# Seven products for q and k in two more pairs of tiles, and what moves between VectorE, ScalarE and Pool with it

## The chip, the cores and the metric

The kernel runs on one core of one Trainium2 chip. The core has TensorE (matrix products, called PE in the profile; its weight loads PEld), VectorE (DVE), ScalarE (ACT), GpSimd (POOL) and SyncE (SP), which here only issues DMAs. Each engine works through its own list of instructions in order, and semaphores make it wait for the others. The metric is the time of one execution in microseconds, as the median of several runs. All times below are microseconds unless marked ns.

## The reference

A layer normalisation, a local attention and a two-layer network on the same normalised input, joined by a gate. Cut to what is computed:

```
xn  = layernorm(x)                                  # x: 2048 x 512
q, k, v = xn @ wqkv                                 # 32 heads of 16
logits[s, w] = q[s] . k[s - 2 w] / 4                # 8 keys, every second position, masked before 0
o   = softmax(logits) over w, times v[s - 2 w]
s   = o @ wo
h   = relu(xn @ w1 + b1) ** 2                       # 1792 wide
g   = silu(h @ w2 + b2)
out = x + s * g
```

b2 is drawn 3.8 times larger than the other biases. All inputs and outputs are float32.

## The kernel before, in words

*Precision.* Every operand of a large product is split in a high part, rounded to the product's format by a ScalarE copy, and a low part, the difference, which VectorE or Pool subtracts. A product of two split operands takes three passes (line 34): high x high, high x low, low x high.

*First stage.* The 2048 rows are 16 tiles of 128. Lines 787 to 793 run over pairs of tiles, (0, 1) ahead of the loop, then a = 2, 4, ... 14, and make q, k and v of both tiles. `pair` (line 730) does it straight: six results of 12 products each, 72 in all. `pair_of_seven` (line 744) makes q and k of the two tiles with seven products of half size (six matrix instructions each, a scheme after Strassen), from four sums of input quarters (`copy_quarter`, `sums`, `high_sums`, `low_sums`, lines 489 to 520) and four sums of weights (the buffers T1 to T4), and then joins the products by two ScalarE copies, five VectorE additions and two Pool additions into the staging tiles `stg`; v stays straight. That is 7 x 6 + 24 = 66. `SEVEN` (line 40) says for which pairs. What is to be done beside pair a for later pairs (transposes of the next tiles, their split, the statistics of tiles further on) is listed by step in `plan` (lines 685 to 718). q, k, v go to DRAM and are loaded again in attention's layout; so do the split inputs (`sx`, `xU`) for later chunks.

*Second stage.* Four chunks c of 512 rows (line 870 on). For each of 14 blocks f of the hidden layer, `up(c, f)` (line 575) makes 12 products into `ph`, ScalarE writes the Relu, the square rounded (`h`, high) and the square in full; in chunk 0 the full square stays in PSUM and VectorE subtracts (`lowh`, line 595), in later chunks it goes to the tile `hf`, of which there is one buffer, and Pool subtracts. Two blocks later `down` (line 802) makes 12 products into the four accumulators `pb`. Between them stand the attention's output products `pw` (`out_product`). When a chunk ends, `gate` (line 847) adds b2 to each `pb` and takes the Silu; `finish` (line 858) multiplies by `pw`, adds x and stores. The order of TensorE at such a boundary is: the last `pb` products, `up` 0 and 1 of the next chunk, one `pw`, `up` 2, and then `pb` with h 0, whose third product is the first that reads a low part.

*Weights of the network.* `next_w` (line 388) prepares one block of w1 and w2: two ScalarE copies, two Pool subtractions, and the load of the raw block two further on. `ahead` (line 720) says at which steps of the first stage blocks are prepared; the rest follow one per step of chunk 0. Blocks that are named in `HOME` (line 38) take a buffer that the first stage used for its weights (Q0 to V1, T1 to T4), and so must wait for that buffer's last use.

*The order on VectorE.* The attention (a generator, line 238) fills what the other work leaves of VectorE: eight units of 256 rows, per unit four times a product of k and q and a reduction, a softmax, and four times a product with v and a reduction. `pump` (line 365) emits its instructions as long as the planner's VectorE clock, which adds a price per instruction (line 61), is not past the TensorE clock plus a margin. `not_before` sets the VectorE clock forward where an instruction depends on TensorE. The engines keep the order of emission, ScalarE's and Pool's too; loads by `dma` alone are placed by the framework. In the softmax's second half (`soft_b`, line 287) VectorE makes the sums and reciprocals and Pool scales `L`.

Of the kernel before, what the change touches and what calls it, by code (L numbers as in the profile page):

```python
# [8 lines left out]
F32 = mybir.dt.float32  # L9
FR = mybir.dt.float32r  # L10
AF = mybir.ActivationFunctionType
# [3 lines left out]
P = 128  # L15
# [10 lines left out]
NCH = S // C  # L26
TPC = C // P
# [7 lines left out]


Q0, Q1, K0, K1, V0, V1, T1, T2, T3, T4 = range(10)
HOME = {0: 10, 1: T1, 2: T2, 3: T3, 4: T4, 5: Q0, 6: Q1, 7: K0, 8: K1, 9: V0, 10: V1}

SEVEN = range(4, 12, 2)  # L40

WARM = 18
WARM2 = 3
# [2 lines left out]

STATS = 6

MATMUL, TRANSPOSE, DVE_FIXED, SLACK, LATE, ROOM0, ROOM = 227, 150, 170, 500, 3000, 500, 3500

BEHIND, FREE, LAND, LOAD = 5000, 2000, 4500, 10500

# [2 lines left out]
def body(ctx: ExitStack, tc: tile.TileContext, x, wqkv, wo, w1, b1, w2, b2, out):  # L55
# [3 lines left out]
    clock = {"PE": 0.0, "V": 0.0}  # L59

    def price(engine, name, a, k):
        if engine == "PE":
            return MATMUL if name == "matmul" else TRANSPOSE
        ap = k["in_"] if name == "tensor_reduce" else k.get("out", a[0] if a else None)
        n = 1
        for d in ap.shape[1:]:
            n *= d
        if name == "reciprocal":
            n *= 8
        return n / 0.96 + DVE_FIXED  # L70

    class Ordered:

# [14 lines left out]
    PE, V, A, G = Ordered(nc.tensor, "PE"), Ordered(nc.vector, "V"), Ordered(nc.scalar), Ordered(nc.gpsimd)  # L88

    def not_before(t):  # L90
        clock["V"] = max(clock["V"], t)
# [3 lines left out]
    def queue(out, in_):  # L95

        tc.keep_in_program_order(dma(out, in_))
# [7 lines left out]
    hpool = ctx.enter_context(tc.tile_pool(name="ph", bufs=1))  # L105
# [5 lines left out]
    def psH(name):  # L111
        return psum.tile([P, 512], F32, name=name, tag="h", bufs=2)

    def psT(name):
        return psum.tile([P, 512], F32, name=name, tag="tp", bufs=2)
# [33 lines left out]
    def buffer(name, i):  # L149
        return wts.tile([P, 2, 2, 512], FR, name=name, tag=f"b{i}")  # L150
# [237 lines left out]
    def next_w():  # L388

        f = len(w12)  # L390
        if f < NF:
            w12[f] = buffer(f"w{f}", HOME[f]) if f in HOME else p2.tile([P, 2, 2, 512], FR, name=f"w{f}")
            for i, r in enumerate(raws.pop(f)):
# [179 lines left out]
    hs = {}  # L573

    def up(c, f):
        ph = psH(f"ph{c}_{f}")
        n = 0
        for kt in range(KT):
            for a, b in PASSES:
                PE.matmul(ph.rearrange("p (j n) -> p j n", n=P), w12[f][:, a, 0, kt * P:(kt + 1) * P],  # L580
                          xT[c][:, :, b, kt, :], start=n == 0, stop=n == 11)
                n += 1
        if f == NF - 1 and c + 1 < NCH:
            load_xT(c + 1)
        h = hpool.tile([P, 2, 512], FR, name=f"h{c}_{f}", tag="h", bufs=3)
        A.activation(ph, ph, AF.Relu, bias=b1t[:, f:f + 1])
        A.activation(h[:, 0], ph, AF.Square)

        full = hpool.tile([P, 512], F32, name=f"hf{c}_{f}", tag="hf") if c else ph
        A.activation(full, ph, AF.Square)  # L590
        if c:
            G.tensor_sub(h[:, 1], full, h[:, 0].bitcast(F32))
        hs[f] = h, None if c else ph, clock["PE"] + 2000

    def lowh(f):
        h, ph, t = hs[f]
        if ph is not None:
            not_before(t)
            V.tensor_sub(h[:, 1], ph, h[:, 0].bitcast(F32))
# [91 lines left out]
    for a in range(2, NT, 2):  # L691
        n, t = (2 if a < 6 else 0), a + 2
        seven = t in SEVEN
        for i in (t, t + 1):
# [22 lines left out]
    for i in range(2):  # L717
        at(4, i, load_w, i)

    ahead = {(4, 4): 1, (12, 4): 2, (14, 4): 2}  # L720

    def beside(a, step):

# [63 lines left out]
    for a in range(2, NT, 2):  # L787
        if a >= TPC:
            for t in (a, a + 1):
                queue(sx[t // TPC][:, t % TPC], xt[t].bitcast(F32))  # L790
        (pair_of_seven if a in SEVEN else pair)(a)
        if a == NT - 4:
# [7 lines left out]
    pws, gs = {}, {}  # L800
# [37 lines left out]
    def out_product(t, ps, cols=slice(0, D)):  # L838
        o = oTs[t]
        n = 0  # L840
        for g in range(4):
            for a, b in PASSES:
                PE.matmul(ps[:, cols], o[:, a, g], wot[:, b, g, cols], start=n == 0, stop=n == 11)
                n += 1
        pws[t] = ps

    def gate(c, j, pb):
        z = gs[c, j] = piece(f"z{c}_{j}")
        V.tensor_add(z, pb[j], b2t)
        A.activation(z, z, AF.Silu)  # L850

    xrs = {}

# [13 lines left out]
    b2t = p2.tile([P, D], F32, name="b2t")  # L867
    rwo = {}

    for c in range(NCH):  # L870
        last = c == NCH - 1
        pb = [psA(f"pb{c}_{j}") for j in range(TPC)]
        t0 = c * TPC
        room = ROOM if c else ROOM0
        for f in range(2, NF):
            up(c, f)
            if c == 0:
                next_w()
            pump()
            if c == 0 and f == 8:  # L880
                dma(b2t, b2[None, :].to_broadcast([P, D]))
            if c == 0 and f in (3, 6):

                i = f // 6
                rwo[i] = p2.tile([P, 2, D], F32, name=f"rwo{i}", tag="oT", bufs=2)
                for q in range(4):
                    rows = wo[q * P + 64 * i:q * P + 64 * i + 64, :].rearrange("(g p) n -> p g n", g=2)
                    dma(rwo[i][32 * q:32 * q + 32], rows)
            if c == 0:
                if 6 <= f < 10:  # L890
                    split(wot[:, 0, f - 6], wot[:, 1, f - 6], rwo[(f - 6) // 2][:, (f - 6) % 2], G)
            elif f == 2:
                finish(t0 - 4, G)
            elif f == 3:
                finish(t0 - 3, G)
                load_r(t0 - 2)
                load_r(t0 - 1)
                trans_o(t0 - 2, psT(f"pT{t0 - 2}"))
                trans_o(t0 - 1, psT(f"pT{t0 - 1}"))
            elif f == 4:  # L900
                lowo(t0 - 2)
                lowo(t0 - 1)
            elif f == 5:
                out_product(t0 - 2, psT(f"pw{t0 - 2}"))
            elif f == 6:
                finish(t0 - 2, G)
                out_product(t0 - 1, psT(f"pw{t0 - 1}"))
            elif f == 7:
                finish(t0 - 1, G)
            if f == 2 and c:  # L910
                load_o(c * 2 - 1, True)
            elif f >= 7:
                load_o(c * 2, f >= 9)
            if f in (9, 10) and not last:
                load_r(t0 + f - 9)
            if f == 10:
                for i in range(2):
                    trans_o(t0 + i, psT(f"pT{t0 + i}"))
            if f == 11:
                for i in range(2):  # L920
                    lowo(t0 + i)
            if f >= 12:
                load_o(c * 2 + 1, last and f > 12)
            if not (last and f == NF - 1):
                for j in range(TPC):
                    down(pb, f - 2, j)
            pump(room)
            lowh(f)
        out_product(t0, psT(f"pw{t0}"))
        if last:  # L930
            out_product(t0 + 1, psT(f"pw{t0 + 1}"))
        pump(room)
        if not last:
            for i in range(2):
                for j in range(TPC):
                    down(pb, NF - 2 + i, j)
                if i == 0:
                    pump(room)
            pump()
            not_before(clock["PE"])  # L940
            for j in range(TPC):
                gate(c, j, pb)
            for i in range(2):
                up(c + 1, i)
                pump(ROOM)
                lowh(i)
            out_product(t0 + 1, psT(f"pw{t0 + 1}"))
            pump(ROOM)
        else:
            for i in range(2, TPC):  # L950
                trans_o(t0 + i, psH(f"pT{t0 + i}"))
            for i in range(2, TPC):
                lowo(t0 + i)
            xl = xTa.tile([P, TPC, 512], F32, name="xlast", tag="xT")
            dma(xl.rearrange("p (h e) n -> p h (e n)", e=2),
                x[t0 * P:(t0 + TPC) * P, :].rearrange("(h p e) n -> p h (e n)", p=P, e=2))
            for j in range(TPC):
                for f in range(NF - 3, NF):
                    down(pb, f, j)
                gate(c, j, pb)  # L960
                if j < 2:
                    finish(t0 + j, V, xl[:, j])
            for j in range(2, TPC):
                n = D // 2 if j == TPC - 1 else D
                for i in range(0, D, n):
                    cols = slice(i, i + n)
                    out_product(t0 + j, (psT if i else psH)(f"pw{t0 + j}_{i}"), cols)
                    finish(t0 + j, V, xl[:, j], cols)
# [21 lines left out]
```

## Time and profile before

| | |
|---|---|
| median of 3 runs | 493.07 (492.94 to 495.27) |
| profiled execution | 492.33 |
| its span, first to last instruction | 490.5 |
| granted TensorE clock | 1.000 of full speed |
| TensorE products in the span | 2130 |

The span is what the views of the trace cover; the 1.83 between it and the time of the same execution lie around it. In a row of instructions "out<-in" names the tiles, "x12" the number merged, and brackets give the idle time of the engine ahead of them and what ended it. All instructions that go through the recording helper have line 84, so they are told apart by their tiles. In the tables of groups the numbers behind "|" are busy us and mean ns of one, then the idle us ahead of them.

### The profile page before, as it was taken

Reading aid. Unit: us, or ns where it says so; the run is one execution under the profiler, and the core shown is the slowest. Engines: PE = TensorE matmul, PEld = TensorE weight load, DVE = VectorE, ACT = ScalarE, POOL = GpSimd, SP = SyncE. Lnnn points to the kernel's source line nnn. Section 1 sums busy time; section 2 is a strip of 40 time slices with the busy share of each in tenths; the row PEclk is TensorE's granted clock in tenths of the full one; section 3 lists DMA queues with packets and bytes.
Section 4 is the critical chain, followed back from the end, with each engine's and each line's share of the span. In section 5 each row is a group of like instructions: output and inputs, shape, how many; then the busy total and the mean of one; then the engine's idle time right before and its main releaser. Section 6 shows DMA issues by size and latency. Waiting matters only on the chain.

```text
span 490.5 us, 5897 instructions
## 1 busy us (share of the span) xinstructions
PE 482.6 (98%) x2130; PEld 396.3 (81%) x2130; DVE 433.5 (88%) x366; ACT 218.0 (44%) x389; POOL 199.6 (41%) x167
## 2 busy tenths in 40 slices
PE   8999999999999999999999999999999999999996
PEld 5887678888888888888888888888888888888886
DVE  5975989899998899999999999999999899979234
ACT  5569387414355557343522424452242445223331
POOL 1415262221469599006444531383643126162210
PEclk9999999999999999999999999999999999999999
DMA  8799969869649976362435409061713915021222
GB/s 288 239 282 299 314 233 313 235 216 382 177 180 297 245 199 226 97 278 79 168 119 168 165 11 358 8 246 51 230 40 130 349 27 203 2 97 33 86 86 87
DMA packets 48521, 88.80 MB, mean 181 GB/s; under 512 B 5372, under 2 KB 32364, under 8 KB 45676
## 3 DMA queue, kind: packets, MB, share of 16 engines
q1 hardware_dynamic: 44172, 54.87, 36.5%
q10 hardware_dynamic: 4320, 33.56, 18.3%
q8 instruction: 17, 0.28, 0.3%
q14 instruction: 12, 0.10, 0.1%
HBM read 57.94 MB, written 27.32 MB: 174 GB/s over the span
## 4 chain that ended last, share of the span: by engine, by line
PE 86%; ACT 1%; issue 1%; DVE 1%; POOL 0%; ACTq 0%
PE ph L84 31%; PE pb L84 31%; PE pq L84 10%; PE pw L84 9%; PE pm L84 5%; POOL stg L84 0%; ACT mean L84 0%; ACT S L84 0%; ACT w L84 0%; ACT var L84 0%; ACT stg L84 0%; DVE z L84 0%; ACT xn L84 0%; DVE Sf L84 0%; DVE pr L84 0%
## 5 line engine op out<-in xcount | busy, mean ns | idle before, releaser
L84 PE MATMUL pb<-w,h 128*128 128x512 f32 x672 | 160.6, 389 | 0.0
L84 PEld LDWEIGHTS pb<-w,h 128*128 128x128 f32 x672 | 126.1, 188 | 26.2
L84 POOL TENSOR_TENSOR h<-hf,h 128x512 fp32r<-128x512 f32 x42 | 73.4, 1748 | 157.7 <-ACT hf L84 153.7
L84 PE MATMUL ph<-xU,w 128*128 128x512 f32 x504 | 120.6, 389 | 0.0
L84 PEld LDWEIGHTS ph<-xU,w 128*128 128x128 f32 x504 | 94.6, 188 | 19.6
L84 ACT ACTIVATE ph<-ph,b1t 128x512 f32<-128x512 f32 x56 | 37.0, 661 | 164.6 <-PE ph L84 155.1
L84 DVE TENSOR_TENSOR pv<-v,L 128x2048 f32<-128x2048 f32 x32 | 79.4, 2481 | 3.9 <-POOL L L84 3.4
L84 DVE TENSOR_TENSOR pr<-k,q 128x2048 f32<-128x2048 f32 x32 | 77.4, 2419 | 0.6
L84 DVE TENSOR_REDUCE L<-pr 128x128 f32<-128x2048 f32 x32 | 73.1, 2283 | 0.7
L84 DVE TENSOR_REDUCE v<-pv 128x256 f32<-128x2048 f32 x32 | 72.9, 2278 | 0.7
L84 PE MATMUL pq<-wq,xt 128*128 128x512 f32 x240 | 56.2, 390 | 0.9 <-DVE stg L84 0.9
L84 PEld LDWEIGHTS pq<-wq,xt 128*128 128x128 f32 x240 | 45.0, 188 | 10.6 <-DVE stg L84 1.3
L84 PE MATMUL pw<-wot,oT 128*128 128x512 f32 (+1 forms) x204 | 45.9, 376 | 0.0
L84 PEld LDWEIGHTS pw<-wot,oT 128*128 128x128 f32 x204 | 36.8, 188 | 7.1
L84 PE MATMUL ph<-xT,w 128*128 128x512 f32 x168 | 40.4, 389 | 0.0
L84 ACT ACTIVATE stg<-pq 128x512 f32<-128x512 f32 x32 | 19.1, 596 | 45.1 <-PE pq L84 40.5
L84 PEld LDWEIGHTS ph<-xT,w 128*128 128x128 f32 x168 | 31.5, 188 | 6.5
L84 ACT ACTIVATE h<-ph 128x512 fp32r<-128x512 f32 x56 | 33.5, 599 | 1.8
L84 POOL TENSOR_TENSOR w<-w1r,w 128x512 fp32r<-128x512 f32 x14 | 23.9, 1705 | 24.4 <-DMA sx<-xt 18.7
L84 PE MATMUL pq<-wq,xT 128*128 128x512 f32 x132 | 30.8, 392 | 0.0
L84 PEld LDWEIGHTS pq<-wq,xT 128*128 128x128 f32 x132 | 24.5, 188 | 5.8 <-ACT xT L84 0.7
L84 PE MATMUL pm<-wq,S 128*128 128x512 f32 x96 | 24.1, 396 | 1.4 <-ACT stg L84 0.8
(80 smaller groups left out, 459.8 us busy)
## 6 DMA issues: line engine op xcount, KB each, us to landing
k<-sk ACTq DMA_DIRECT2D x8, 1408.0 KB, 6.8
v<-sv ACTq DMA_DIRECT2D x8, 1408.0 KB, 8.9
sx<-xt SPq DMA_DIRECT2D x12, 512.0 KB, 6.1
xU<-sx ACTq DMA_DIRECT2D x6, 1024.0 KB, 6.8
x<-in_A_x SPq DMA_DIRECT2D x16, 256.0 KB, 4.0
sk<-stg SPq DMA_DIRECT2D x8, 512.0 KB, 3.9
sq<-stg SPq DMA_DIRECT2D x8, 512.0 KB, 4.7
q<-sq ACTq DMA_DIRECT2D x8, 512.0 KB, 7.1
```

Of the source, the lines that this page charges most:

```text
L84: return tc.keep_in_program_order(f(*a, **k))
```

## The change

- `SEVEN` covers pairs 12 and 14 too, so all tiles from 4 on get q and k by seven products a pair.
- In chunks 0 to 2 ScalarE copies each `pb` to z, Pool adds b2, and the Silu of all four z stands in ScalarE's order behind the activations of the next chunk's `up` 0 and 1. The last chunk keeps VectorE's addition.
- In chunk 0 the low parts of h 0, 1, 12 and 13 are made as in later chunks: full square to `hf`, difference on Pool.
- The planner prices a VectorE instruction 20 ns lower and a large `tensor_mul` 200 ns higher; the VectorE clock is no longer set forward at the gate.
- Weight blocks take other buffers (`HOME`), block 1 is prepared at pair 6, and blocks 2 and 3 at pair 14: four blocks are prepared before chunk 0 begins its steps, where there were five.

```diff
-HOME = {0: 10, 1: T1, 2: T2, 3: T3, 4: T4, 5: Q0, 6: Q1, 7: K0, 8: K1, 9: V0, 10: V1}
-SEVEN = range(4, 12, 2)
+HOME = {0: 10, 1: K0, 2: Q0, 3: T1, 4: T2, 5: Q1, 6: T3, 7: K1, 8: V0, 9: V1, 10: T4}
+SEVEN = range(4, 16, 2)
...
-MATMUL, TRANSPOSE, DVE_FIXED, SLACK, LATE, ROOM0, ROOM = 227, 150, 170, 500, 3000, 500, 3500
+MATMUL, TRANSPOSE, DVE_FIXED, SHARED, SLACK, LATE, ROOM0, ROOM = 227, 150, 150, 200, 500, 3000, 500, 3500
...
-        return n / 0.96 + DVE_FIXED
+        return n / 0.96 + DVE_FIXED + (SHARED if name == "tensor_mul" and n >= 2048 else 0)
...
-        full = hpool.tile([P, 512], F32, name=f"hf{c}_{f}", tag="hf") if c else ph
+        pool = c or f < 2 or f > 11
+        full = hpool.tile([P, 512], F32, name=f"hf{c}_{f}", tag="hf") if pool else ph
         A.activation(full, ph, AF.Square)
-        if c:
+        if pool:
             G.tensor_sub(h[:, 1], full, h[:, 0].bitcast(F32))
-        hs[f] = h, None if c else ph, clock["PE"] + 2000
+        hs[f] = h, None if pool else ph, clock["PE"] + 2000
...
-    ahead = {(4, 4): 1, (12, 4): 2, (14, 4): 2}
+    ahead = {(4, 4): 1, (6, 4): 1, (14, 4): 2}
...
     def gate(c, j, pb):
         z = gs[c, j] = piece(f"z{c}_{j}")
-        V.tensor_add(z, pb[j], b2t)
-        A.activation(z, z, AF.Silu)
+        if c == NCH - 1:
+            V.tensor_add(z, pb[j], b2t)
+            silu(c, j)
+        else:
+            A.activation(z, pb[j], AF.Copy)
+            G.tensor_add(z, z, b2t)
+
+    def silu(c, j):
+        A.activation(gs[c, j], gs[c, j], AF.Silu)
...
             pump()
-            not_before(clock["PE"])
             for j in range(TPC):
                 gate(c, j, pb)
             for i in range(2):
                 up(c + 1, i)
                 pump(ROOM)
                 lowh(i)
+            for j in range(TPC):
+                silu(c, j)
             out_product(t0 + 1, psT(f"pw{t0 + 1}"))
```

## The prediction

> **What bounds the kernel now.** I read the page first, then the chain of waits in order of time, TensorE's own timeline for its gaps, the busy time by stretches, and the groups of instructions by shape.
>
> ```profile
> span 490.5 us, 5897 instructions
> PE 482.6 (98%) x2130; PEld 396.3 (81%) x2130; DVE 433.5 (88%) x366; ACT 218.0 (44%) x389; POOL 199.6 (41%) x167
> ```
>
> TensorE is busy for 98% of the span. Its last gap on TensorE's timeline is this one (start, duration, what, and in brackets the gap before it):
>
> ```profile
> 66.07 3.03 PE L84 MATMUL pm<-wq,S 128*128 128x512 f32 x12 [0.81 <-ACT stg L84]
> ```
>
> From there to the last product it never waits. The chain (start, duration) shows the regular pace; these rows are the change from chunk 0 to chunk 1, the same place one chunk on, and the end:
>
> ```profile
> 211.90 5.44 PE pb L84 x24
> 217.34 5.44 PE ph L84 x24
> ...
> 228.22 2.72 PE pb L84 x12
> ...
> 304.38 5.44 PE ph L84 x24
> ...
> 481.18 5.60 PE pw L84 x36
> ```
>
> 24 products take 5.44, so one costs 0.2267 us. What is taken from TensorE comes off the span, as long as every other engine still delivers in time. The nearest of these is VectorE:
>
> ```profile
> 146.00:212.00 66.00, 66.00 (x293) 54.65 (x292) 60.21 (x42) 36.07 (x62) 44.28 (x28) 1.00 0.73 226
> 212.00:299.00 87.00, 87.00 (x385) 72.04 (x384) 86.04 (x55) 32.70 (x54) 37.41 (x22) 1.00 0.39 142
> ```
>
> (Columns: busy PE, weight loads, VectorE, ScalarE, Pool, then clock and DMA.) VectorE has 1 us free out of 87 in a chunk, and 5.8 out of 66 in chunk 0. So the kernel has two engines at their limit, and the change loads one while it relieves the other.
>
> **The change, part by part.**
>
> *Products.* Pairs 12 and 14 each go from 72 to 66 products. 12 x 0.2267 = 2.72 us come off TensorE, certain as far as nothing waits. The gaps before 69 us stay: up to pair 6 the instructions of TensorE and VectorE keep their order.
>
> *VectorE work of these pairs.* Per pair four sums, two low parts of sums and five additions into the staged q and k; what is taken away are a sum with b2 for twelve tiles and four low parts of h:
>
> ```profile
> L84 DVE TENSOR_TENSOR stg<-stg,pm 128x512 f32<-128x512 f32 x20 | 13.2, 678 | 1.9 <-ACT xt L84 1.5 <-POOL stg L84 0.2
> L84 DVE TENSOR_TENSOR z<-pb,b2t 128x512 f32<-128x512 f32 x16 | 10.4, 685 | 2.2 <-PE pb L84 2.1
> L84 DVE TENSOR_TENSOR h<-ph,h 128x512 fp32r<-128x512 f32 x14 | 9.5, 679 | 4.7 <-ACT ph L84 3.6 <-PE pb L84 1.1
> L84 DVE TENSOR_TENSOR S<-Sf,S 128x512 fp32r<-128x512 f32 x8 | 5.7, 712 | 2.8 <-ACT S L84 2.8
> L84 DVE TENSOR_TENSOR Sf<-pxT,Sf 128x256 f32<-128x256 f32 x8 | 3.4, 421 | 0.1
> ```
>
> Added: 2 x (4 x 0.421 + 2 x 0.712 + 5 x 0.678) = 13.0 us, all before chunk 0. Removed: 12 x 0.685 + 4 x 0.679 = 10.9 us, but one boundary at a time: before the first boundary only two low parts, 1.4. So VectorE is nearly balanced over the kernel and up to 11.6 us late when chunk 0 ends. Where that shows is the attention's second softmax half (sums, reciprocal, then a scaling of L on Pool). Its reciprocals stand here, with a reduction that I use below:
>
> ```profile
> 201.81 0.55 DVE L84 RECIPROCAL sm_None<-sm_None 128x64 f32<-128x64 f32 x1
> ...
> 219.04 2.28 DVE L84 TENSOR_REDUCE L<-pr 128x128 f32<-128x2048 f32 x1
> ...
> 293.41 0.55 DVE L84 RECIPROCAL sm_None<-sm_None 128x64 f32<-128x64 f32 x1
> ```
>
> *The sums with b2 on Pool.* Each chunk boundary gets four Pool additions, and in Pool's order they stand ahead of the low part of the next chunk's h 0. At the first and second boundary the scaling of L stands ahead of them too. A Pool addition alone takes 1.29; beside a VectorE product it does not run:
>
> ```profile
> 137.61 2.28 DVE L84 TENSOR_TENSOR pv<-v,L 128x2048 f32<-128x2048 f32 x1
> ...
> 227.20 2.87 DVE L84 TENSOR_TENSOR pv<-v,L 128x2048 f32<-128x2048 f32 x1
> ```
>
> ```profile
> 137.77 3.06 POOL L84 TENSOR_TENSOR L<-L,mx_None 128x512 f32<-128x512 f32 x1 [10.02 <-DVE mx_None L84]
> ...
> 226.83 1.08 POOL L84 TENSOR_TENSOR L<-L,mx_None 128x512 f32<-128x512 f32 x1
> ...
> 231.36 1.29 POOL L84 TENSOR_TENSOR z<-z,xr 128x512 f32<-128x512 f32 x1
> ```
>
> The L operation costs 1.08 when it starts first, and then the product stretches to 2.87; it costs 3.06 when the 2.28 product starts first. So they take turns. While VectorE alternates product and reduction (2.3 each), a Pool with a backlog gets two additions per 2.28 + 2 x 1.29 = 4.9 us. [...]
>
> Now the first boundary. Call T the end of chunk 0's last `pb` product (217.34 before, 214.62 after). The last four groups of three products end 0.68 apart, the first at T-2.0, and a copy takes 0.6, so z comes from T-1.4 on. TensorE wants the low part of h 0 at the third product of `pb`: 228.22 - 217.34 + 2 x 0.23 = T+11.3. Pool has six operations until then (L, four z, h 0). The reciprocal ended at 202.36; plus 13.0, less 1.4, less what chunk 0's 5.8 idle us take up: 208.2 to 214.0, which is T-6.4 to T-0.7. With it at T-0.7 the next product starts at once, L is through at T+2.7, and turn by turn come z at 4.0, 7.5, 8.8, 12.5 and h 0 at 13.8: TensorE waits 2.5. With it at T-3.2 or earlier, h 0 is there in time: 0. I take T-2, a wait of 1.2, as Pool's collisions in chunk 0 speak for the late end.
>
> The second boundary depends on the first. ScalarE's second copy of h 1 needs the single `hf` buffer back from Pool's h 0, and behind it in ScalarE's order now stand the table load and the four Silus:
>
> ```profile
> 209.17 1.28 ACT L84 ACT_TABLE_LOAD   x1
> ...
> 217.36 2.43 ACT L84 ACTIVATE z<-z 128x512 f32<-128x512 f32 x4 [6.91 <-DVE z L84]
> ...
> 224.83 0.60 ACT L84 ACTIVATE hf<-ph 128x512 f32<-128x512 f32 x1 [0.72 <-POOL h L84]
> ```
>
> So VectorE's z x pw waits for h 0, a copy, the table load and one Silu, and with its own 0.7 it ends 3.2 after h 0, at T+14.6 plus the wait s that TensorE had; VectorE stops for up to 5 us. From the reduction at 219.04 to the reciprocal's end at 293.96 VectorE needed 74.9, without the z product in it 74.3. Added, that gives T+88.9+s; the next boundary T2 is at T+87.04+s (304.38 - 217.34): the reciprocal comes 1.8 after T2, and by the same turns, with two products ahead of z x pw, h 0 comes 12.2 after the reciprocal, at T2+14.0: a wait of 2.7. If VectorE doesn't stop, it reaches T2 1.7 early and nothing waits. Between 0 and 2.7 I take 1.5. At the third boundary L stands behind h 0; five operations from T-1.4 at 2.45 end at T+10.9: 0.
>
> *One weight block fewer in advance.* Before, block 5 is prepared in chunk 0's first step, now block 4. Block 5's first low part ended at 153.72 and was read at 160.22:
>
> ```profile
> 150.37 3.35 POOL L84 TENSOR_TENSOR w<-w1r,w 128x512 fp32r<-128x512 f32 x1 [0.84 <-ACT w L84]
> ```
>
> ```profile
> 160.22 2.72 PE ph L84 x12
> ```
>
> 6.5 us of margin less one step (two rows of 2.72, 5.44) leave 1.1: cost 0, and up to 2 if Pool is late by one blocked operation more.
>
> *Block 1 at pair 6.* Two ScalarE copies (1.2 us) stand ahead of the staged q of pair 8. Behind them ScalarE idles in any case:
>
> ```profile
> 79.92 0.60 ACT L84 ACTIVATE stg<-pm 128x512 f32<-128x512 f32 x1 [2.03 <-DMA sk<-stg]
> ```
>
> The 2.03 cover them. On the SP queue the two loads of block 3 now wait for Pool ahead of q's and v's stores and four shuffles, which come later by at most a blocked and a free operation (3.06 + 1.29); the shuffled tiles are first read a pair (66 x 0.2267 = 15 us) on. Cost 0; without that cover up to 1.2.
>
> *Planner's prices, Copy instead of an addition on ScalarE, buffers' new homes.* They move work in VectorE's order and cost nothing by themselves; the four copies (0.60 each) per boundary fit ScalarE's 6.91 idle.
>
> *Attention's end.*
>
> ```profile
> 451.19 2.29 DVE L84 TENSOR_REDUCE v<-pv 128x256 f32<-128x2048 f32 x1
> ...
> 463.99 0.73 DVE L84 STREAM_TRANSPOSE pT<-oq 128x512 f32<-128x512 f32 x1 [7.93 <-ACT hf L84]
> ```
>
> It ended at 453.5 and its tiles were multiplied from 481.18 on; store and load took at most 10.5 of these 27.7. Even 12 us later fits: 0.
>
> *Sum.* -2.72 + 1.2 + 1.5 = 0.0 on the profiled 492.33 (span 490.5 and 1.83 around it). The median 493.07 is 0.74 above that execution; on it the forecast is 493.1.
>
> **The rivals.**
>
> *No wait at all.* For it: TensorE has had none from 69 us on, and VectorE can catch up in chunk 0's 5.8 idle us. Against it: six Pool operations in 12.6 us. Time: 493.07 - 2.72 = 490.35.
>
> *VectorE's lateness grows from boundary to boundary* (slower). Place: h 0 behind L and four z on Pool. Price: each us that the reciprocal comes later is a us of TensorE. It decides from 5.2 us of waits on: with the reciprocals 2 us later than my late bounds, 4.5 + 4.7 = 9.2, less 2.72 = +6.5: 499.6; with exactly the late bounds, 2.5 + 2.7 less 2.72 = +2.5: 495.6. For it: 86.04 busy of 87.00. Against: each chunk loses 2.7 us of b2 sums.
>
> *Weights late in chunk 0.* The margin of 1.1 goes in several of ten steps: with 1 us in each, 10 - 2.72: about 500. Against: ScalarE and Pool still idle in chunk 0 (36.07 and 44.28 of 66).
>
> **How the numbers follow.** Forecast (the gain given back at the boundaries) 0.40, no wait 0.32, growing lateness 0.20, weights 0.08. A difference of 0.5% (2.47 us) is what a measurement here can tell from none. Faster: the no-wait case and 0.02 of the forecast, 0.34. Slower: 0.19 + 0.07 and 0.02 of the forecast, 0.28. The rest, 0.38, within. The range 490.0 to 498.0 holds the no-wait case with a little noise and most of the third. The forecast's own range is 490.4 to 495.6.
>
> **What would show it.** Right: TensorE's products 12 fewer, gaps of 0.5 to 3 us in `pb` at the first and second boundary released by Pool's h, z x pw on VectorE idle for about 5 us on ScalarE's Silu, Pool's additions with b2 at 3.3 every other time. Wrong: no gap there; or gaps in `ph` of chunk 0 released by Pool's w; or new gaps in `pm` of pairs 8 to 14, which I price at nothing.

## The result, and the profile after

The changed kernel takes 499.05 (median of 6 runs, 497.25 to 502.04), the kernel before 493.0 beside it (6 runs, 492.69 to 495.27): a ratio of 1.0122 with an interval of 1.0101 to 1.0143. It is 6 us slower, where 493.1 had been forecast. The profiled execution took 498.9, its span is 497.0. The page has it so (the span, then busy time of each engine):

```profile
span 497.0 us, 5943 instructions
PE 483.0 (97%) x2118; PEld 394.2 (79%) x2118; DVE 442.4 (89%) x372; ACT 224.2 (45%) x403; POOL 247.7 (50%) x187
```

TensorE has 12 products fewer, as said, and yet is busy for longer than before (482.6). TensorE's own timeline after 70 us shows why: three places where it now waits or runs slowly, none of them there before.

```profile
179.44 0.73 PE L84 MATMUL ph<-xT,w 128*128 128x512 f32 x2
180.80 2.56 PE L84 MATMUL ph<-xT,w 128*128 128x512 f32 x10 [0.62 <-POOL w L84]
183.20 2.88 PE L84 MATMUL pb<-w,h 128*128 128x512 f32 x12
185.92 3.26 PE L84 MATMUL ph<-xT,w 128*128 128x512 f32 x12
189.02 2.88 PE L84 MATMUL pb<-w,h 128*128 128x512 f32 x12
...
227.51 0.61 PE L84 MATMUL pb<-w,h 128*128 128x512 f32 x2
229.52 2.56 PE L84 MATMUL pb<-w,h 128*128 128x512 f32 x10 [1.40 <-POOL h L84]
231.92 2.88 PE L84 MATMUL ph<-xU,w 128*128 128x512 f32 x12
...
316.24 0.61 PE L84 MATMUL pb<-w,h 128*128 128x512 f32 x2
320.34 3.56 PE L84 MATMUL pb<-w,h 128*128 128x512 f32 x10 [3.49 <-POOL h L84]
323.70 3.54 PE L84 MATMUL ph<-xU,w 128*128 128x512 f32 x12
327.09 2.88 PE L84 MATMUL pb<-w,h 128*128 128x512 f32 x12
```

Such rows are best read from start to start: 12 products that keep pace take 2.72. From 179.44 to 183.20 they took 3.76, from 185.92 to 189.02 3.10, and one row like it at 191.74 took 3.12.

| place | more than the pace | of it waiting, by the brackets |
|---|---|---|
| low parts of weights late, 179 to 195 | 1.04 + 0.38 + 0.40 = 1.82 | 0.62 |
| first boundary, `pb` with h 0 | 4.41 - 2.72 = 1.69 | 1.40 |
| second boundary, `pb` with h 0 | 7.46 - 2.72 = 4.74 | 3.49 |
| the `ph` behind it | 3.39 - 2.72 = 0.67 | none |
| 12 products fewer | -2.72 | |

Together 8.92 - 2.72 = 6.2, and the same place at 66 us comes 0.24 later than before: 6.44 of the 6.5 that the spans differ by.

The 0.67 of the `ph` row is no waiting at all. In the busy time by stretches (PE, weight loads, VectorE, ScalarE, Pool, then granted clock, DMA share and rate) the clock falls behind the long gap:

```profile
320.30:322.00 1.70, 1.66 (x7) 1.34 (x7) 0.00 (x0) 1.66 (x2) 1.00 (x1) 0.89 0.00 0
322.00:324.00 2.00, 2.00 (x6) 1.62 (x5) 1.11 (x2) 1.99 (x5) 0.27 (x1) 0.50 0.00 0
324.00:326.00 2.00, 2.00 (x8) 1.54 (x8) 1.97 (x2) 1.97 (x4) 0.00 (x0) 0.74 0.00 0
326.00:328.00 2.00, 2.00 (x11) 1.65 (x10) 2.00 (x1) 0.77 (x3) 1.84 (x2) 1.00 0.00 0
```

Six and eight products fall into 2 us, where the last stretch, at full clock, has 11. The 22 products behind the gap take 3.36 + 3.39, where 22 x 0.2267 = 4.99: 1.76 us on top of the 3.65 by which the gap moved their start.

Now what the two boundaries waited for, from the timelines of VectorE and Pool (T = 216.63 is the end of chunk 0's last `pb` product, T2 = 305.36 that of chunk 1):

```profile
217.37 0.55 DVE L84 RECIPROCAL sm_None<-sm_None 128x64 f32<-128x64 f32 x1
...
308.43 0.55 DVE L84 RECIPROCAL sm_None<-sm_None 128x64 f32<-128x64 f32 x1
...
322.89 0.69 DVE L84 TENSOR_TENSOR z<-z,pw 128x512 f32<-128x512 f32 x1 [3.86 <-ACT z L84]
```

```profile
218.00 3.00 POOL L84 TENSOR_TENSOR L<-L,sm_None 128x512 f32<-128x512 f32 x1 [7.07 <-DVE sm_None L84]
221.15 7.10 POOL L84 TENSOR_TENSOR z<-z,b2t 128x512 f32<-128x512 f32 x4
228.22 1.25 POOL L84 TENSOR_TENSOR h<-hf,h 128x512 fp32r<-128x512 f32 x1
...
309.07 3.01 POOL L84 TENSOR_TENSOR L<-L,sm_None 128x512 f32<-128x512 f32 x1 [10.38 <-DVE sm_None L84]
312.03 7.04 POOL L84 TENSOR_TENSOR z<-z,b2t 128x512 f32<-128x512 f32 x4
319.03 1.26 POOL L84 TENSOR_TENSOR h<-hf,h 128x512 fp32r<-128x512 f32 x1
```

Pool works almost without a break from the reciprocal to h 0, 11.5 us the first time (217.92 to 229.47) and 11.3 the second. So TensorE's wait is set by when VectorE has the reciprocal: at T+1.3 and at T2+3.6, where the kernel before had it 15 and 10 us ahead of these ends.

### The profile page after: what moved, and what is told of

Read it like the earlier page. It is cut to its first block, busy times and chain, and to the rows that moved or that the text cites. A ratio compares the mean times of both kernels' runs of the same rounds, so it can differ in the third digit from the quotient of the medians.

```text
span 497.0 us, 5943 instructions
## 1 busy us (share of the span) xinstructions
PE 483.0 (97%) x2118; PEld 394.2 (79%) x2118; DVE 442.4 (89%) x372; ACT 224.2 (45%) x403; POOL 247.7 (50%) x187
## 4 chain that ended last, share of the span: by engine, by line
PE 64%; POOL 7%; issue 7%; DMA 5%; DVE 4%; ACT 2%; ACTq 0%; SPq 0%; POOLq 0%
PE pb L84 21%; PE ph L84 20%; PE pm L84 10%; PE pw L84 7%; PE pq L84 6%; POOL w L84 3%; DVE v L84 2%; POOL z L84 2%; DVE pv L84 2%; DMA w1r<-in_B_w 2%; POOL h L84 2%; DMA rwo<-in_A_wo 1%; DMA so<-v 1%; DMA w2r<-in_B_w 1%; DVE pr L84 0%
## 5 line engine op out<-in xcount | busy, mean ns | idle before, releaser
L84 POOL TENSOR_TENSOR h<-hf,h 128x512 fp32r<-128x512 f32 x46 | 77.3, 1680 | 100.2 <-ACT hf L84 95.2
L84 DVE TENSOR_TENSOR pr<-k,q 128x2048 f32<-128x2048 f32 x32 | 86.9, 2716 | 1.4 <-DMA q<-sq 0.9
L84 DVE TENSOR_TENSOR pv<-v,L 128x2048 f32<-128x2048 f32 x32 | 78.0, 2438 | 3.3 <-POOL L L84 2.6
L84 PE MATMUL pm<-wq,S 128*128 128x512 f32 x144 | 35.6, 394 | 1.3 <-ACT stg L84 0.8
L84 PE MATMUL pq<-wq,xt 128*128 128x512 f32 x144 | 34.7, 390 | 0.9 <-DVE stg L84 0.9
L84 ACT ACTIVATE hf<-ph 128x512 f32<-128x512 f32 x46 | 27.4, 595 | 16.8 <-POOL h L84 16.8
L84 PEld LDWEIGHTS pm<-wq,S 128*128 128x128 f32 x144 | 26.6, 188 | 8.8 <-ACT stg L84 1.4
L84 PEld LDWEIGHTS pq<-wq,xt 128*128 128x128 f32 x144 | 26.9, 188 | 6.9 <-DVE stg L84 1.3
L84 ACT ACTIVATE stg<-pq 128x512 f32<-128x512 f32 x24 | 14.3, 594 | 36.8 <-PE pq L84 33.5
```

The lines of the kernel that those rows point to most:

```text
L84: return tc.keep_in_program_order(f(*a, **k))
```

## The experiments

All times are medians beside runs of the kernel before in the same series (492.84 to 493.04). Theory L is that VectorE's lateness, brought on by the sums for seven products, decides. Its chief rival is that the additions of b2 on Pool decide by themselves.

**Less work on VectorE ahead of the first boundary.** Everything stays in the changed kernel but four instructions on VectorE: two products with v and their two reductions are left out, and with them a part of the attention's result.

```diff
-                if u > 1 or (u == 0 and s < 2) or (u == 1 and s >= 2):
+                if (u > 1 and (u, s) not in ((2, 2), (2, 3))) or (u == 0 and s < 2) or (u == 1 and s >= 2):
```

> The changed kernel with two products and two reductions over the values (the second half of rows 256 to 511, the attention's unit 1) left out: about 9.3 us of VectorE's work less, all just ahead of the first boundary's reciprocal; nothing else changes place except what follows in VectorE's order. Theory L (VectorE's lateness decides): the first boundary's reciprocal ends at about T-8 instead of T+1.3 and the second's at about T2-5 instead of T2+3.6, so both waits in front of pb (1.4 and 3.5 us) are under 0.3 us, the slower products behind them go too, and with the weights' gap at 180 us left the time is 499.05 - 1.55 - 3.65 - 1.5 to 2.0 = 491.8 to 492.5. Rival Q (four additions ahead of h 0 on Pool are enough however early L is): the waits stay above 1 us each, 495.5 or more.

Measured: 492.08 (491.19 to 494.9, 10 runs), ratio 0.9987 (0.9969 to 1.0004). The timelines of VectorE and TensorE:

```profile
209.02 0.55 DVE L84 RECIPROCAL sm_None<-sm_None 128x64 f32<-128x64 f32 x1
```

```profile
181.72 2.56 PE L84 MATMUL ph<-xT,w 128*128 128x512 f32 x10 [0.62 <-POOL w L84]
...
228.40 2.88 PE L84 MATMUL pb<-w,h 128*128 128x512 f32 x12
...
315.44 2.88 PE L84 MATMUL pb<-w,h 128*128 128x512 f32 x12
```

The reciprocal ends 8 us ahead of this chunk's end (217.52), and `pb` with h 0 is an unbroken row of 12 at both boundaries, although L and the four additions still stand ahead of h 0. The time falls by 6.97; the table above puts 1.69 + 4.74 + 0.67 = 7.10 on the boundaries. The wait for weights stays. So the lateness decides, not the additions by themselves. But they leave little room: in this run, with L long done, Pool's h 0 ends at 228.39, and the third product of `pb`, which reads it, is due at 228.85.

**The sums with b2 back on VectorE.**

```diff
-        if c == NCH - 1:
-            V.tensor_add(z, pb[j], b2t)
-            silu(c, j)
-        else:
-            A.activation(z, pb[j], AF.Copy)
-            G.tensor_add(z, z, b2t)
+        V.tensor_add(z, pb[j], b2t)
+        silu(c, j)
```

The later loop over `silu` goes, and VectorE's clock is set forward ahead of the gate again.

> The changed kernel with one part undone: the sums with b2 are VectorE's again and the Silu follows at once, as before the change; seven products, homes, low parts of h on Pool and the prices stay. Theory Q (Pool's queue): what TensorE waited for at the first two boundaries was h 0 behind L and four additions on Pool. Without the additions only L stands ahead of h 0 (about 1.1 to 3.1 us), so both waits (1.4 and 3.5 us in front of pb) and the slower products behind them go: 499.05 - 1.55 - 3.65 - 1.5 to 2.5 = about 491.3 to 492.4, with the wait for block 9's weights (about 0.9 us) still there. VectorE then carries 12 x 0.685 = 8.2 us more, so rival L (VectorE's lateness as such): the waits go to other places, the sums with b2 themselves or the attention's end, and the time stays at 496 to 500.

Measured: 501.06 (500.43 to 501.34, 4 runs), ratio 1.0151 (1.0127 to 1.0176). The waits of Pool's h at the boundaries are gone, and theory Q's number is missed by 9 us; rival L holds in kind, one us above its range. VectorE's last reduction of the attention and the end of TensorE's timeline:

```profile
474.51 2.29 DVE L84 TENSOR_REDUCE v<-pv 128x256 f32<-128x2048 f32 x1
```

```profile
486.51 7.46 PE L84 MATMUL pw<-wot,oT 128*128 128x512 f32 x36 [3.77 <-DVE oT L84]
```

The attention ends 23 us later than in the kernel before (451.19), and its tiles come too late for the last products: a wait of 3.77, and 36 products in 7.46 where they took 5.60. The moved sums are what spares the changed kernel this; its own attention ends at 467.7. The run shows one thing more. The first two reciprocals end as late as in the changed kernel (219.07 and 310.43), and yet no product waits for Pool's h; the first boundary has only a wait of 0.66 for ScalarE's hf. So it takes both for the changed kernel's waits at the boundaries, a late reciprocal and the four additions ahead of h 0.

**The moved sums alone, in the kernel before.** The edit is the gate of the change with nothing else of it.

> The kernel before with one part of the change alone: ScalarE copies the four blocks at a boundary, Pool adds b2, the Silu comes behind h 0 and h 1. Theory Q with L early: in the kernel before the reciprocals end at T-15 and T2-10, so the scaling of L is through before the additions start; four additions in turns with VectorE's products take about 10 us from T-1.4, h 0 comes at T+9 to T+10, before TensorE's third product at T+11.3: no wait, and the time is that of the kernel before, 492.5 to 493.5. Rival G (the additions on Pool are enough by themselves, however early L is): waits of 1 us or more at each boundary, 495 or more. VectorE is relieved by 8.2 us in either case.

Measured: 498.27 (497.61 to 499.48, 4 runs), ratio 1.0099 (1.0066 to 1.0131), which is in rival G's range, but without what rival G is about: no boundary waits for Pool. TensorE's timeline has one gap, and ScalarE's queue shows what was late:

```profile
395.80 7.35 PE L84 MATMUL ph<-xU,w 128*128 128x512 f32 x24 [3.73 <-DMA xU<-sx]
```

```profile
382.26 0.52 ACTq L84 DMA_DIRECT2D v<-sv  x1
382.88 1.03 ACTq L84 DMA_DIRECT2D xU<-sx  x2
```

In the kernel before the two stand the other way round:

```profile
380.57 1.11 ACTq L84 DMA_DIRECT2D xU<-sx  x2
...
383.03 0.53 ACTq L84 DMA_DIRECT2D v<-sv  x1
```

With less for VectorE to do, the planner emits the attention's load of v (1408 KB) earlier, just ahead of the load of the next chunk's x (two of 1024 KB), and v itself must wait, by the order of the program, for a store of an earlier result: x goes out at 382.88, where it went out at 380.57. To tell this from the additions, the loads were held over the last step of a chunk; that swaps the two at the third boundary and changes no other place in the order:

```diff
+    hold = [False]
...
-        while behind and (t is None or behind[0][0] <= t):
+        while not hold[0] and behind and (t is None or behind[0][0] <= t):
...
+            hold[0] = f == NF - 2 and not last
             pump(room)
+            hold[0] = False
             lowh(f)
```

> The kernel before with the moved sums with b2 alone, as in the run of that part by itself (498.27), but with the loads of q, k and v held back over the last step of a chunk, which changes one thing in the order: at the third boundary the load of the next chunk's x stands ahead of the load of v on ScalarE's queue again, as in the kernel before. Theory D (the 3.73 us wait at 392 us was for that load alone, and the 24 products behind it, 7.35 instead of 5.44, were slow because of the wait): no gap there, 498.27 - 3.73 - 1.9 = 492.6, within 0.5 of the kernel before. Rival G (the additions on Pool cost a wait by themselves): a wait for Pool's h or ScalarE's hf comes in its place, 494.5 or more.

Measured: 493.09 (492.48 to 495.05, 10 runs), ratio 1.0002 (0.9989 to 1.0015), no gap after 70 us. The moved sums cost nothing while VectorE is early, and gain nothing.

**All parts but the seven products.** `SEVEN`, `HOME` and `ahead` of before in the changed kernel.

> The changed kernel without its seven products: pairs 12 and 14 by nine products as before, with the weights' homes and advance of before; the moved sums with b2, four more low parts of h on Pool and the planner's prices stay. The load of the next chunk's x stands ahead of that of v at every boundary. Theory L (without the 13 us of sums VectorE isn't late, and the other parts cost nothing): no waits above 0.5 us after 70 us, 492.0 to 493.5. Rival P (the low parts of h on Pool or the prices cost by themselves): gaps in chunk 0 or at the boundaries, 494.5 or more.

Measured: 492.9 (492.13 to 494.77, 10 runs), ratio 0.9995 (0.9981 to 1.0009), no gap after 70 us. Prices, low parts of h on Pool and moved sums are worth nothing together. The loss needs the two pairs, with the weights' buffers and times that go with them.

**The order at the boundary.** First only Pool's additions go behind h 0 and h 1; then the Silus too go behind ScalarE's copies of h 2.

```diff
             A.activation(z, pb[j], AF.Copy)
-            G.tensor_add(z, z, b2t)
...
                 lowh(i)
             for j in range(TPC):
+                G.tensor_add(gs[c, j], gs[c, j], b2t)
                 silu(c, j)
```

> The changed kernel with Pool's four additions of b2 moved behind the low parts of h 0 and h 1; everything else as changed. Theory Q: only L stands ahead of h 0, which comes about 4 to 5 us behind the reciprocal, at T+6 to T+9: no wait of TensorE at the boundaries, 491.3 to 493. The Silus and z x pw come later, by what four additions take (5 to 10 us). Rival Z (z x pw on VectorE then stops VectorE for longer than before, and VectorE is later from boundary to boundary): gaps at the second boundary or at the finishing of tiles, 494 to 497.

Measured: 498.14 (497.39 to 498.75, 4 runs), ratio 1.0093 (1.0068 to 1.0119). The list of TensorE's waits (total, times, longest) no longer has Pool's h, but this in its place:

```profile
PE ph L84 <- ACT hf L84: 4.0, 3, 1.8
```

ScalarE stands at the first Silu, which waits for Pool's addition, and behind it stand its copies of h 2. The wait moved by one engine, and both forecasts, 493 at most and 497 at most, are missed. So, with the additions where they now are:

```diff
             for j in range(TPC):
                 G.tensor_add(gs[c, j], gs[c, j], b2t)
-                silu(c, j)
...
             up(c, f)
+            if c and f == 2:
+                for j in range(TPC):
+                    silu(c - 1, j)
```

> The changed kernel with Pool's four additions of b2 behind the low parts of h 0 and h 1, as in the run that gave 498.14 with waits of 1.5, 1.8 and 0.7 us for ScalarE's hf, and with the four Silus moved behind ScalarE's copies of h 2 besides (loads of q, k, v held back over a chunk's last step). Theory S (in that run ScalarE stood at a Silu that waited for Pool's addition, and the copies of h 2 stood behind it): the Silus no longer stand ahead of h 2, so no wait over 0.3 us at the three boundaries although VectorE is as late as in the changed kernel; what is left is the waits for weights between 180 and 195 us (1.8 to 2.1 in all): 493.04 - 2.72 + 1.8 to 2.3 = 492.1 to 492.6. Rival L2 (VectorE's lateness shows elsewhere once the boundaries don't hold TensorE up: at the finishing of tiles or at the attention's end): 494 to 497.

Holding the loads back changes no place in the order here. Measured: 494.52, but from 492.21 to 497.34 over 10 runs; ratio 1.0029 (1.0009 to 1.0049). The boundaries are free of waits. One of 1.18 for VectorE's oT is new, as rival L2 had it in kind, and theory S's number is missed by 2 us. The profile is of the slowest run and shows what made that one slow: the weights' wait, and half clock behind it (TensorE's timeline, then the stretch).

```profile
182.75 0.74 PE L84 MATMUL ph<-xT,w 128*128 128x512 f32 x2 [1.02 <-ACT w L84]
184.11 4.14 PE L84 MATMUL ph<-xT,w 128*128 128x512 f32 x10 [0.62 <-POOL w L84]
```

```profile
186.00:188.00 2.00, 2.00 (x6) 1.63 (x5) 2.00 (x3) 1.48 (x3) 2.00 (x2) 0.50 0.25 70
```

That doesn't explain the whole spread: the other nine runs have a mean granted clock of 0.998 to 1.000 and still take from 492.21 to 495.56. What spreads them stays open.

**Weights.** In the changed kernel block 9's raw weights are loaded from 170.39 on, since their load stands on SP's queue behind the attention's `oq`, which waits for a store (3.3 us in the list of waits); ScalarE has them at 178.75. One more block in advance was tried at two places: three blocks in step 4 of the last pair, and one each behind steps 1, 2 and 4.

```diff
-    ahead = {(4, 4): 1, (6, 4): 1, (14, 4): 2}
+    ahead = {(4, 4): 1, (6, 4): 1, (14, 4): 3}
```

> The changed kernel with one more weight block prepared in the last pair (five ahead instead of four, as in the kernel before). Theory W (one block fewer in advance made block 9 late): TensorE's gap at 180 us, released by Pool's low part of w (0.6 us in the list of waits, 0.9 start to start), and the slower products behind it (0.9 in all) go: 497.2 to 498.2, the two gaps at the boundaries stay within 1 us of 1.4 and 3.5. Rival (block 9 is late because its load stands on SP's queue behind stores and loads that wait for the attention, so one block more in hand only moves the gap to block 10 or is not felt): 498.7 to 499.5 and the gap still there.

```diff
-    ahead = {(4, 4): 1, (6, 4): 1, (14, 4): 2}
+    ahead = {(4, 4): 1, (6, 4): 1, (14, 1): 1, (14, 2): 1, (14, 4): 1}
```

> The changed kernel with five weight blocks in advance, prepared one each behind the steps 1, 2 and 4 of the last pair (the run with three in step 4 gave 501.91, with waits for Pool's h at 149 us). Theory W: the three waits for weights at 180, 186 and 192 us (1.0, 0.4 and 0.4 us) go and none comes at 140 to 150; the waits at the first two boundaries stay at 1.4 and 3.5 within 1 us: 496.9 to 498.0. Rival: Pool's low parts of the weights and of h 0 get in each other's way wherever the block is put, 498.5 or more.

Measured: 501.91 (497.78 to 502.55, 4 runs; ratio 1.0153, 1.0106 to 1.02) for three at once, 498.31 (494.28 to 499.9, 5 runs; ratio 1.0091, 1.0059 to 1.0124) spread. With three at once, Pool's low part of h comes late at the start of chunk 0, as neither theory had it, and the clock falls there:

```profile
148.92 4.14 PE L84 MATMUL pb<-w,h 128*128 128x512 f32 x10 [2.78 <-POOL h L84]
```

```profile
149.00:151.00 2.00, 2.00 (x5) 1.54 (x6) 0.00 (x0) 1.97 (x4) 1.27 (x1) 0.54 0.27 94
```

Spread out, the three waits between 179 and 195 us are gone and none comes at 149, as theory W had it; its number is missed by 0.3, near the rival's 498.5. Its median moved by 0.7 with a spread of 5.6, and the profile, of its fastest run, has no wait at the second boundary; so the gain of 1.8 that the table suggests is seen in the rows, not proved by the median.

**Versions that beat both.** One takes seven products for pair 12 only, in the kernel before, with the moved sums and the load of x ahead of v:

```diff
-SEVEN = range(4, 12, 2)
+SEVEN = range(4, 14, 2)
-    ahead = {(4, 4): 1, (12, 4): 2, (14, 4): 2}
+    ahead = {(4, 4): 1, (14, 1): 2, (14, 4): 2}
```

> A middle way, put together from the parts: the kernel before with seven products in pair 12 alone (6 products, 1.36 us, less), the moved sums with b2, x ahead of v on ScalarE's queue, and the first four weight blocks prepared in the last pair. Theory L: VectorE gets 6.5 us more ahead of chunk 0 and 2.7 less at each boundary, the first reciprocal comes at about T-8, the second at T2-4: no wait at the boundaries, 493.0 - 1.4 = 491.6, or 491.3 to 492.2. Rival W (four blocks of weights prepared in one pair make Pool late for h 0 to h 1 or for block 3 to 5 in chunk 0): gaps in ph or pb between 135 and 160 us, 493 to 496.

Measured: 491.22 (491.13 to 491.32, 5 runs), ratio 0.9959 (0.9946 to 0.9972). No wait after 70 us, as theory L had it. The page has:

```profile
span 489.5 us, 5926 instructions
```

The same with one block fewer, `(14, 4): 1`:

> The middle way (491.22) with four weight blocks in advance instead of five, nothing else changed. Theory W: waits for Pool's w of 0.5 to 2.5 us in all come back in ph between 160 and 200 us, 491.7 to 493.7. Rival (the late loads of blocks 9 to 11 in the changed kernel come from the order on SP's and ScalarE's queues alone, which this kernel has otherwise): no wait, 491.0 to 491.5.

Measured: 491.55 (491.01 to 493.1, 10 runs), ratio 0.9969 (0.9953 to 0.9985), no wait either, as the rival had it. Four blocks are enough where the loads come in time. The last version keeps both pairs, with late additions, late Silus and the five blocks spread out:

> As the kernel with late additions and late Silus, and five weight blocks in advance instead of four, prepared one each behind the steps 1, 2 and 4 of the last pair. Theory W (the waits for weights between 180 and 195 us come from the margin of one block): they go as well, so that nothing waits after 70 us: 490.3 to 491.0. Rival (Pool is late for h 0 and h 1 of chunk 0 or for a later block instead): gaps of 1 us or more between 140 and 200 us, 491.5 to 494.

Measured: 491.89 (491.44 to 493.76, 12 runs), ratio 0.998 (0.9967 to 0.9993). That is 0.9 above theory W's range; the number is in the rival's, but not its place. One wait with a releaser is left:

```profile
330.80 3.02 PE L84 MATMUL pw<-wot,oT 128*128 128x512 f32 x12 [1.23 <-DVE oT L84]
```

It costs 1.39 up to its end and 0.14 behind it. The spans add up: 490.5 - 2.72 + 1.53, with 0.38 for a short stop at 223 us and 0.30 by which this run is later already at 66 us, is 490.0, the span of this run. So the products are worth what was said, once nothing waits.

## Why the prediction was wrong, point by point

*Products.* Right: 12 fewer, -2.72, seen whole in the spans of the last version with both pairs.

*VectorE's added work.* Right in itself, wrong in what follows. Groups of VectorE from 69 us to the reciprocal, before and after:

```profile
L84 DVE TENSOR_TENSOR pr<-k,q 128x2048 f32<-128x2048 f32 x10 | 24.0, 2404 | 0.2
L84 DVE TENSOR_TENSOR stg<-stg,pm 128x512 f32<-128x512 f32 x14 | 9.2, 677 | 1.5 <-ACT xt L84 1.5
```

```profile
L84 DVE TENSOR_TENSOR pr<-k,q 128x2048 f32<-128x2048 f32 x10 | 27.7, 2769 | 1.1 <-DMA q<-sq 0.9
L84 DVE TENSOR_TENSOR stg<-stg,pm 128x512 f32<-128x512 f32 x24 | 16.0, 679 | 3.4 <-DMA sk<-stg 1.7 <-PE pq L84 1.2 <-PE pm L84 0.2
```

The additions into stg cost 6.8 more, as reckoned (10 x 0.678). But the same ten products of k and q cost 3.7 more. Seven of the ten took 2.51 to 3.44, where two had before (2.59 and 3.10) and the others 2.27 to 2.35. That more of them run beside Pool's work is the likely reason: in the changed kernel one beside Pool's additions took 3.42 (at 222.42) and one with Pool idle 2.28 (at 323.50), and in the stretches below Pool is busy for 89.69 of 148.40 us, against 68.96 of 132.80. And the idle time was not used up. The stretches to the reciprocal:

```profile
69.00:201.80 132.80, 132.80 (x588) 109.96 (x587) 125.73 (x109) 67.90 (x128) 68.96 (x51) 1.00 0.77 242
```

```profile
69.00:217.40 148.40, 147.62 (x648) 120.99 (x647) 139.18 (x131) 70.72 (x134) 89.69 (x59) 1.00 0.73 232
```

VectorE's idle time is 132.80 - 125.73 = 7.07 before and 148.40 - 139.18 = 9.22 after. Most of it is time in which VectorE waits for others: 5.9 and 7.6 of it have a releaser by the list of waits, and after the change waits for a store (1.7), for TensorE (1.4) and for a load (0.9) are new. So VectorE is 15.6 us later at the reciprocal, by 13.45 of work, where 11.6 had been reckoned, and by 2.15 of idle time, where up to 5.8 were to be won back. The prediction had "208.2 to 214.0" for the reciprocal, its late end with none of the idle time saved; it came at 217.92. This is the step that failed, the term "less what chunk 0's 5.8 idle us take up": nothing was taken up. The reciprocal is 3.9 us beyond the late bound in absolute time, 2.0 counted from T (which the weights made 2.0 later), and the forecast's T-2 is missed by 3.3.

*Turns on Pool.* Too dear: from the reciprocal to h 0 14.5 us had been reckoned, 11.5 were measured. VectorE started one long product within the four additions (at 222.42, 3.42) and the next only as they ended (at 228.20), where the count had two among them. The copies of `pb` were no help: ScalarE made them at 220.41 and not from T-1.4 on, behind a load of v into a buffer whose earlier content had to be stored first (that store was issued at 216.77 and took 3.0 to land, which is when the load starts; the bracket puts the wait down to VectorE). ScalarE's timeline:

```profile
219.82 0.54 ACTq L84 DMA_DIRECT2D v<-sv  x1
220.41 2.07 ACT L84 ACTIVATE z<-pb 128x512 f32<-128x512 f32 x4 [11.80 <-DVE pr L84]
```

Pool was at L until 221.0, so that cost next to nothing here. The two errors, 3.3 late and 3.0 short, nearly cancel at the first boundary, by luck: a wait of 1.40 (1.69 with the restart) for the predicted 1.2.

*Second boundary.* Mis-sized: 1.5 taken, 2.7 as the upper bound, 5.41 measured, of which 3.65 is the gap and 1.76 the clock behind it. Against the prediction's 1.2, 1.5 and 0 (weights) the table above has 1.69, 5.41 and 1.82, so this term is 3.9 of the 6 us. Its two parts were both wrong. VectorE's z x pw does stand for the Silu, for 3.86, but at the second boundary; at the first, where a long product filled the time, it stood 0.52 and not up to 5. And the relief of 2.7 a chunk by the moved sums was not there: from one reciprocal to the next VectorE took 91.6 before and 91.06 after. The two nearly cancel, again by luck: from T+1.3 to T2+3.6 the reciprocal fell back by 2.3, where the late bound had it fall back by 2.5, so the error at the second boundary is the one carried over from the first. The products of k and q and those with v of that stretch, eight of each, before and after:

```profile
L84 DVE TENSOR_TENSOR pr<-k,q 128x2048 f32<-128x2048 f32 x8 | 20.0, 2495 | 0.2
L84 DVE TENSOR_TENSOR pv<-v,L 128x2048 f32<-128x2048 f32 x8 | 18.8, 2355 | 0.1
```

```profile
L84 DVE TENSOR_TENSOR pr<-k,q 128x2048 f32<-128x2048 f32 x8 | 22.4, 2798 | 0.2
L84 DVE TENSOR_TENSOR pv<-v,L 128x2048 f32<-128x2048 f32 x8 | 20.3, 2534 | 0.2
```

VectorE got rid of 2.5 for the four sums and 1.4 for the low parts of h 12 and 13 there, 3.9 in all, and the longer products took back 2.4 + 1.5 = 3.9. (In the kernel before with the moved sums and x ahead of v, the same stretch took 90.1, from 201.97 to 292.07: 1.5 of the 2.7 were left.) A chunk is 87 us of TensorE, so this stretch takes VectorE 4 us or more longer, before as after; the kernel before could bear it with its 15 us in hand, and its next stretch took 86.9.

*Price of a wait.* Taken at its own length. The long one cost 1.76 more on its 3.65, by the clock (see the last section).

*Weights.* The margin did go, not at block 5 by a blocked operation but at block 9 with a late load. The sum took 0; 1.82 was measured, near the end of "up to 2".

*Third boundary, block 1 at pair 6, prices.* Right: no gap there in the changed kernel, and the run without the two pairs shows prices and moved sums at nothing. *Attention's end.* "Even 12 us later fits" held at 14 (467.7 for 453.5); with 23 it doesn't, by the run with the sums on VectorE.

*Which case.* It was the rival "VectorE's lateness grows from boundary to boundary", with its reciprocal 2 us beyond the late bound as that rival's first price had it, and its 499.6 lies by the 499.05. That is in part luck, as it came there by another sum: 7.1 at the boundaries for 9.2, and 1.8 from the weights. The chance of 0.20 was too low, since the row 86.04 of 87.00 was weighed less than a catching up that no row showed.

## What to carry to other kernels

When work goes from a full engine to another that is nearly full, don't set it off against that engine's idle time: idle time on an engine that keeps its order can be waiting for others. Here it mostly was (5.9 of 7.07 us before, 7.6 of 9.22 after), and it grew as the engine fell late. Add it to the time of the one instruction on whose result others wait, here a small reciprocal, and follow that through the next engine's queue to the first product that needs it. And run a relief for its side effects too: it can move the loads that are emitted by the planner's clock of the relieved engine, and here one such move brought a wait of 3.73.

## What the runs showed of the hardware that was not expected

Behind some gaps of TensorE the granted clock falls to half: 1.3 us after TensorE went on behind the gap of 3.49 (at 320.34, the fall by 321.6) and 0.2 after it behind the one of 2.78 (at 148.92, the fall by 149.2). Each time the clock stays there for about 3.4 us. This is an estimate from the mean clock of the stretches, taking it that the clock is either full or half, as it is behind the gap of 3.49 in stretches of 0.2 us (1.00 up to 321.60, 0.50 from 321.80 to 325.00, 1.00 from 325.20 on): (0.11 x 1.70 + 0.50 x 2 + 0.26 x 2) / 0.5 = 3.4 behind the gap of 3.49, and (0.46 + 0.40) x 2 / 0.5 = 3.4 behind the one of 2.78 (the 0.54 shown, then 0.60). So a fall cost the same here, however long the gap was: 1.76 us behind 3.49, 1.74 behind 3.73 (24 products in 7.18 in place of 5.44), 1.72 behind 2.78 (10 in 3.99 in place of 2.27), 1.73 behind 1.78 in the run with three blocks at once (22 in 6.72 in place of 4.99), and 1.73 behind 0.42 and 1.84 with 3 us between them (22 in 6.72 again), in the run with the blocks spread out. Behind the 3.73 and the 1.78 the fall is read from the products' pace alone; the mean granted clocks of these two executions, 0.996 and 0.993, fit one fall and two (3.4 x 0.5 / 500 = 0.0034 each). The row behind the 1.84:

```profile
228.81 3.57 PE L84 MATMUL pb<-w,h 128*128 128x512 f32 x10 [1.84 <-POOL h L84]
```

In one run it fell behind gaps of 1.02 and 0.62 (shown above), while gaps of 0.85 and 0.62 in the kernel with the sums back on VectorE, or single ones of 1.40 in the changed kernel and of 1.54 and 1.79 in the one with Pool's additions behind h 0 and h 1, left the next row nearly at pace (2.40 for 10 products behind the 0.62 and behind the 1.40, 2.85 and 2.86 for 12 behind the 1.54 and the 1.79). So whether a gap of 1 to 2 us brings a fall is not told by its length alone: 1.78 brought one, 1.79 did not.

That the clock falls in some executions of a kernel and less, or not at all, in others is a likely reason for the spread of the changed kernel's runs (497.25 to 502.04). The mean granted clock goes with it at the ends, 1.000 in the fastest and 0.992 in the two slowest, and 0.8% of 500 us is 4 of the 4.8 us between the extremes. It was not tried by itself, and in the kernel with the blocks spread out the clock doesn't tell the runs apart: it was 0.997 in the fastest (494.28) as in the slowest (499.9).
